# Packed attention with a feed-forward network: the first batch runs alone through all inner chunks

## The chip, the cores and the metric

The kernel runs on one core of a Trainium2 chip. The metric is the device time of one execution in microseconds (us), median of the runs. TensorE (PE) multiplies matrices into PSUM banks; VectorE (DVE), ScalarE (ACT) and GpSimd (POOL) work element by element; SyncE (SP) issues the transfers.

## The reference, cut to what matters

```python
def sm_attn(qq, kk, vv):                       # per batch and head
    s = scale * np.matmul(qq, kk.transpose(0, 1, 3, 2))
    s = s - np.max(s, axis=-1, keepdims=True)
    a = np.exp(s)
    a = a / (np.sum(a, axis=-1, keepdims=True) + 1e-09)
    return np.matmul(a, vv)
p_packed = sm_attn(p, k, v)                    # 32 packed rows per head
out = sm_attn(q, p_packed, p_packed)           # 576 tokens per head
...
h = x @ w_in                                   # x: 4608 x 512, w_in: 512 x 2048
g = h * (1.0 / (1.0 + np.exp(-1.702 * h)))
return (g @ w_out).astype(np.float32)          # w_out: 2048 x 512
```

There are 8 batches, 8 heads, 576 tokens a batch, heads of 64; the weights are float64 in memory.

## The kernel before, in words

All work is written out as one list of steps, `order` (from line 675), which is run from the top; it sets each engine's order. Engines meet only by semaphores. For a batch `b` the steps are:

- `load` brings k and the packed rows, q and v. Their tiles share two buffers, so q of a batch waits until k of it is used.
- `scores1`, the first softmax (`max1_first`, `bias1`, `exp1`, `sum1`), `turn1` (PE transposes the exps in 128-column pieces, plus the last 64) and `pack` (line 352) make the packed rows P; `pack_turn` transposes them to `PT`. Each exists for even and odd heads (`eo` 0 and 1).
- `scores2_mm`, `scores2_turn`, `max2`, `sub2`, `exp2`, `sum2`, `norm2`, `turn2` make the second softmax for one half of the tokens (288, `half` 0 and 1), both parities side by side in a tile of 576 columns.
- `m_chunk` (line 385) multiplies PT by one of four column chunks of w_in (512 columns), for even and odd heads in two banks. So the attention's product with w_in is never made in full: an `h_mm` step (line 539) multiplies the second softmax by that m.
- Every operand that is multiplied is split into an upper part that PE takes in its fast form and a lower part, the rest: `a_upper`/`a_lower`, `m_upper`/`m_lower`, `h_upper`/`h_lower` (tiles ghi, glo), `upper_w`/`lower_w`. One `h_mm` step is six matmuls of 288 columns for one 128-row slice `f` (16 of them) and one half of the tokens; one `out_mm` step is three matmuls of 512 columns for one `f` and one block of 128 tokens (four of them). In the head some lower parts are made by PE itself, with an identity and a negated identity, and copied (`a_lower_mm`, tile psal; `lower_w_mm`, tile pswl).
- `h_tanh` (ACT) and `h_gate` (DVE) make the gate. The last 64 tokens of each batch are kept aside (`h_over`) and multiplied for two batches at once (`over_mm`), then copied (`over_take`) and stored (`over_store`).

The weights come as 32 blocks of 128 rows in 64-bit form: 16 of w_in (four per chunk) and 16 of w_out (one per `f`), numbered as they are needed. `load_w` fetches a block, `begin_w` (ACT) and `join_w` (DVE) make 32-bit numbers of it; a block of w_out then needs `upper_w` and `lower_w`.

In the kernel before, the first two batches take turns. The table `spans` (line 663) lets batch 0 run chunk 0, batch 1 chunks 0 and 1, batch 0 chunks 1 to 3 and batch 1 chunks 2 and 3. The unfinished sums of a span are stored in device memory (`aside`) and fetched back (`back`) to be added at the end. So the attention of batch 1 stands in the head as well, between the first steps of batch 0. Where PE has nothing to do there, `warm` steps (line 121) multiply the identity by itself, with no use of the result. Every `warm` matmul shows as two instructions in the profile.

```python
spans = [(0, 0, 1), (1, 0, 2), (0, 1, 4), (1, 2, 4)]
```

Of the kernel before, what the change touches and what calls it, by code (L numbers as in the profile page):

```python
# [21 lines left out]
def kernel(  # L22
# [31 lines left out]

# [19 lines left out]
    DEC = 3  # L74
    SCALE = 1.0 / float(D) ** 0.5
# [6 lines left out]
    dram = ctx.enter_context(tc.tile_pool(name="dram", bufs=1, space=bass.MemoryType.DRAM))  # L82
# [90 lines left out]
    def load_w(n):  # L173
        w = queue[n]
        i = slot_of(w)
        if w[0] == "in":
            src, at = w_in_raw[w[2] * P : (w[2] + 1) * P, :], 4 * w[1] * FC
        else:
            src, at = w_out_raw[w[1] * P : (w[1] + 1) * P, :], 0
        raw[i] = wk.tile([P, DM, 2], U32, tag=f"wo{i}", name=f"raw{i}")  # L180
        halves = raw[i].rearrange("p n w -> p (n w)").bitcast(U16)
        nc.sync.dma_start(halves[:, : 4 * DM - 1], src[:, at + 1 : at + 4 * DM])
# [7 lines left out]
    tops = [cst.tile([P, DM], U32, name=f"top{i}") for i in range(DEC)]  # L190
# [5 lines left out]
    def begin_w(n):  # L196
        top[n] = tops.pop(0)
        nc.scalar.copy(
            top[n].bitcast(F16).rearrange("p (n h) -> p n h", h=2)[:, :, 1],
            raw[slot_of(queue[n])].bitcast(BF16).rearrange("p n (w h) -> p n w h", h=2)[:, :, 1, 0],  # L200
        )

    def join_w(n):
        w = queue[n]
        if w[0] == "in":
# [3 lines left out]
        nc.vector.scalar_tensor_tensor(  # L209
            dec[n].bitcast(U32), raw[slot_of(w)][:, :, 0], 13, top[n],  # L210
            op0=ALU.logical_shift_right, op1=ALU.bitwise_or,
        )
        tops.append(top[n])
# [138 lines left out]
    def pack(b):  # L352

        aT, vt = st["aT", b], kq["v", b]
        bank = bank_b(f"pspv_{b}")
        bv = bank[:, : 2 * D].rearrange("p (e d) -> p e d", d=D)
        for eo in range(2):
            for c in range(KC):
                kk = P if c < KC - 1 else KLAST
                for j in range(NP):  # L360
                    e0 = (2 * j + eo) * D
                    nc.tensor.matmul(  # L362
                        bv[32 * j : 32 * j + 32, eo, :],
                        aT[:kk, c, eo, 32 * j : 32 * j + 32],
# [20 lines left out]
    def m_chunk(b, fc, banks=(bank_b, bank_b)):  # L385

        PT = st["PT", b]
        banks = [bank(f"psm_{b}_{fc}_{eo}") for eo, bank in enumerate(banks)]
        for j in range(NP):
            for eo in range(2):  # L390
                nc.tensor.matmul(  # L391
                    banks[eo][32 * j : 32 * j + 32, :],
                    PT[rows(eo), j, :],
                    w_in_sb[fc][rows(eo), j, :],
                    start=True,
                    stop=True,
                )
        st["bank", "m", b, fc] = banks

    def m_upper(b, fc, eo, engine=nc.scalar):  # L400
        bank = st["bank", "m", b, fc][eo]
        hi = wk.tile([P, FC], F32R, tag=f"mhi{eo}", name=f"mhi_{b}_{fc}_{eo}", bufs=2)
        move(engine, hi, bank)
        st["m", b, fc, eo] = [hi, bank]

    def m_again(b, fc, banks):

        PT = st["PT", b]
        st["again", b, fc] = banks = [bank(f"psma_{b}_{fc}_{i}") for i, bank in enumerate(banks)]
        for j in range(NP):  # L410
            for eo in range(2):
                nc.tensor.matmul(
                    banks[eo][32 * j : 32 * j + 32, :],
                    PT[rows(eo), j, :],
                    w_in_sb[fc][rows(eo), j, :],
                    start=True,
                    stop=False,
                )
        for eo in range(2):
            hi = st["m", b, fc, eo][0]  # L420
            nc.tensor.matmul(banks[eo], minus, hi, start=False, stop=True)

    def m_again_copy(b, fc, eo, engine=nc.scalar):
        m = st["m", b, fc, eo]
        m[1] = wk.tile([P, FC], F32R, tag=f"mlo{eo}", name=f"mlo_{b}_{fc}_{eo}", bufs=2)
        move(engine, m[1], st["again", b, fc][eo])

    def m_lower(b, fc, eo):
        hi, bank = m = st["m", b, fc, eo]
        m[1] = wk.tile([P, FC], F32R, tag=f"mlo{eo}", name=f"mlo_{b}_{fc}_{eo}", bufs=2)  # L430
        nc.vector.tensor_tensor(m[1], bank, hi.bitcast(F32), op=ALU.subtract)  # L431
# [50 lines left out]
    def norm2(b, half):  # L482
        key = (2, b, half)
        x, rs = st["x", *key], st["rs", *key]
        nc.vector.tensor_tensor(groups(x), groups(x), over(rs), op=ALU.mult)

    def turn2(b, half):
        st["t", 2, b, half] = t = x_tile(f"xt_{b}_{half}")
        nc.vector.transpose(t, st["x", 2, b, half])

    def a_upper(b, half, engine=nc.scalar):
        t = st["t", 2, b, half]
        hi = wk.tile([P, S], F32R, tag="ahi", name=f"ahi_{b}_{half}", bufs=4)
        lo = wk.tile([P, S], F32R, tag="alo", name=f"alo_{b}_{half}", bufs=4)
        move(engine, hi, t)
        st["a", b, half] = (hi, lo)

    def a_lower_mm(b, half, banks):

        hi, lo = st["a", b, half]  # L500
        for eo in range(2):
            at = slice(eo * NH, (eo + 1) * NH)
            st["al", b, half, eo] = bank = banks[eo](f"psal_{b}_{half}_{eo}")
            t = st["t", 2, b, half][:, at]
            nc.tensor.matmul(bank[:, :NH], ident, t, start=True, stop=False)  # L505
            nc.tensor.matmul(bank[:, :NH], minus, hi[:, at], start=False, stop=True)

    def a_lower_copy(b, half, engine=nc.scalar):
        lo = st["a", b, half][1]
        for eo in range(2):  # L510
# [875 lines left out]
```

## Time and profile before

| what | value |
|---|---|
| median of 3 runs | 717.47 us (716.63 to 718.25) |
| the profiled execution, its own time | 716.67 us |
| span of the profiled execution | 714.9 us |
| PE busy | 706.4 us, 99% |
| DVE, ACT, POOL busy | 411.5, 271.9, 138.7 us |
| bytes moved by transfers | 60.06 MB |

The span runs from the first to the last instruction of the program; the own time holds what lies around it too. A row of instructions in time order gives its start, how long its group lasted, the engine, the source line, the operation, the tiles (out<-in), the shape and the count. A group by line or form gives the total busy time and the mean of one in ns, then the idle time before.

### The profile page before, as it was taken

How to read it: one execution, taken by the hardware profiler on the slowest of the kernel's cores; microseconds unless marked ns; L12 is line 12 of the kernel's file. 1: busy time of each engine (PE TensorE's matmuls, PEld its weight loads, DVE VectorE, ACT ScalarE, POOL GpSimd, SP SyncE). 2: the span in 40 equal slices, each digit the busy share in tenths (PEclk: the TensorE clock that was granted, in tenths of full speed). 3: DMA queues.
4: the chain of work that ended last, by engine and by line, in shares of the span. 5: the costliest groups of instructions: out<-in, count | busy, mean ns of one | idle time of the engine just before them, and what ended most of it. 6: DMA issues, size and time to landing. Idle time of an engine off the chain costs nothing.

```text
span 714.9 us, 13041 instructions
## 1 busy us (share of the span) xinstructions
PE 706.4 (99%) x5115; PEld 576.1 (81%) x5115; DVE 411.5 (58%) x1022; ACT 271.9 (38%) x653; POOL 138.7 (19%) x177
## 2 busy tenths in 40 slices
PE   8999999999999999999999999999999999999997
PEld 6678887887878878888887788888787887878885
DVE  4898766765834255335635467543673637855543
ACT  3666554533224344444223333442232333233330
POOL 1042222112232143322141112201241100000000
PEclk9999999999999999999999999999999999999999
DMA  8879063114122202121100400413013110010001
GB/s 315 323 280 349 34 244 119 33 47 147 51 83 71 70 2 107 53 67 71 67 16 1 123 26 1 143 35 119 1 23 110 37 54 1 1 60 0 1 11 63
DMA packets 18619, 60.06 MB, mean 84 GB/s; under 512 B 2176, under 2 KB 2176, under 8 KB 17536
## 3 DMA queue, kind: packets, MB, share of 16 engines
q1 hardware_dynamic: 18560, 59.25, 23.7%
q8 instruction: 40, 0.66, 0.4%
q14 instruction: 19, 0.16, 0.1%
HBM read 47.70 MB, written 11.53 MB: 83 GB/s over the span
## 4 chain that ended last, share of the span: by engine, by line
PE 96%; DVE 2%; DMA 1%; ACT 0%; POOL 0%; issue 0%; SPq 0%; DVEq 0%; ACTq 0%
PE acc L607 49%; PE h L547 29%; PE acc_over L607 6%; PE psm L391 4%; PE pspv L362 2%; PE ps L240 1%; PE ps L440 1%; PE pst L330 1%; PE warm L125 1%; DMA k<-pk 1%; PE psal L505 0%; POOL glo L534 0%; DVE wo L222 0%; DVE mx L287 0%; ACT x L117 0%; DVE aT L119 0%
## 5 line engine op out<-in xcount | busy, mean ns | idle before, releaser
L607 PE MATMUL acc<-wo,ghi 128*128 128x512 f32 x1024 | 323.7, 397 | 0.0
L607 PEld LDWEIGHTS acc<-wo,ghi 128*128 128x128 f32 x1024 | 179.8, 188 | 41.2 <-issue 14.9
L555 ACT ACTIVATE g<-h 128x288 f32<-128x288 f32 x256 | 103.8, 410 | 258.3 <-PE h L547 227.2
L607 PE MATMUL acc<-wo,glo 128*128 128x512 f32 x512 | 201.7, 394 | 0.1
L534 POOL TENSOR_TENSOR glo<-g,ghi 128x288 fp32r<-128x288 f32 (+1 forms) x153 | 115.5, 764 | 423.3 <-ACT ghi L117 221.4
L537 DVE SCALAR_TENSOR_TENSOR g<-g,h 128x288 f32<-128x288 f32 (+1 forms) x256 | 104.7, 415 | 129.0 <-ACT g L555 128.0
L547 PE MATMUL h<-ahi,mhi 128*128 128x288 f32 x512 | 145.8, 299 | 0.7 <-DVE g L537 0.4
L547 PE MATMUL h<-ahi,mlo 128*128 128x288 f32 x512 | 143.3, 295 | 0.0
L607 PEld LDWEIGHTS acc<-wo,glo 128*128 128x128 f32 x512 | 96.1, 188 | 23.4 <-POOL glo L534 1.1
L547 PE MATMUL h<-alo,mhi 128*128 128x288 f32 x512 | 110.3, 297 | 0.0
L547 PEld LDWEIGHTS h<-ahi,mhi 128*128 128x128 f32 x512 | 96.2, 188 | 17.1 <-DVE x L451 2.9
L547 PEld LDWEIGHTS h<-ahi,mlo 128*128 128x128 f32 x512 | 96.2, 188 | 7.0
L117 ACT CAST ghi<-g 128x288 fp32r<-128x288 f32 (+1 forms) x160 | 63.1, 406 | 61.0 <-DVE g L537 46.8
L547 PEld LDWEIGHTS h<-alo,mhi 128*128 128x128 f32 x512 | 82.1, 188 | 0.1
L537 DVE SCALAR_TENSOR_TENSOR over<-g,h 128x64 f32<-128x64 f32 x128 | 27.3, 214 | 65.7 <-ACT g L555 65.4
L534 DVE TENSOR_TENSOR glo<-g,ghi 128x224 fp32r<-128x224 f32 (+1 forms) x103 | 42.9, 425 | 12.1 <-ACT ghi L117 7.9
L431 DVE TENSOR_TENSOR mlo<-psm,mhi 128x512 fp32r<-128x512 f32 x64 | 43.1, 683 | 4.4 <-ACT mhi L117 4.0
L607 PE MATMUL acc_over<-wo,ghi_over 128*128 128x512 f32 x128 | 39.8, 392 | 0.0
L119 DVE CAST ghi<-g 128x224 fp32r<-128x224 f32 (+1 forms) x96 | 29.6, 314 | 13.4 <-PE acc_over L607 7.1
L391 PE MATMUL psm<-w_in,PT 64*32 64x512 f32 x512 | 35.5, 597 | 0.0
L117 ACT CAST mhi<-psm 128x512 fp32r<-128x512 f32 x44 | 25.3, 587 | 23.2 <-PE psm L391 23.1
L607 PEld LDWEIGHTS acc_over<-wo,ghi_over 128*128 128x128 f32 x128 | 23.6, 188 | 4.9 <-issue 0.2
(85 smaller groups left out, 494.1 us busy)
## 6 DMA issues: line engine op xcount, KB each, us to landing
q<-q SPq DMA_DIRECT2D x16, 576.0 KB, 5.4
v<-v SPq DMA_DIRECT2D x8, 1024.0 KB, 6.6
raw<-w_in SPq DMA_DIRECT2D x16, 511.8 KB, 10.4
raw<-w_out SPq DMA_DIRECT2D x16, 511.8 KB, 5.8
o<-o SPq DMA_DIRECT2D x24, 256.0 KB, 2.3
k<-pk SPq DMA_DIRECT2D x8, 640.0 KB, 4.4
k<-pk SPq DMA_DIRECT2D x8, 576.0 KB, 6.2
aside<-o SPq DMA_DIRECT2D x8, 256.0 KB, 4.5
```

Of the source, the lines that this page charges most:

```text
L117: nc.scalar.copy(dst, src)
L119: engine.tensor_copy(dst, src)
L125: nc.tensor.matmul(t[:, :P], ident, ident, start=True, stop=True)
L240: nc.tensor.matmul(bank[32 * j : 32 * j + 32, :NH], kq["p", b][rows(eo), j, :], kq["k", b][rows(eo), half, j, :], start=True, stop=True,)
L362: nc.tensor.matmul(bv[32 * j : 32 * j + 32, eo, :], aT[:kk, c, eo, 32 * j : 32 * j + 32], vt[:kk, c, e0 : e0 + D], start=(c == 0), stop=(c ...
L391: nc.tensor.matmul(banks[eo][32 * j : 32 * j + 32, :], PT[rows(eo), j, :], w_in_sb[fc][rows(eo), j, :], start=True, stop=True,)
L431: nc.vector.tensor_tensor(m[1], bank, hi.bitcast(F32), op=ALU.subtract)
L534: engine.tensor_tensor(lo, src, hi.bitcast(F32), op=ALU.subtract)
L537: nc.vector.scalar_tensor_tensor(dst, th, 1.0, h, op0=ALU.add, op1=ALU.mult)
L547: nc.tensor.matmul(h[:, :NH], m[eo][part][:, fo : fo + P], a[:, eo * NH : (eo + 1) * NH], start=(n == 0), stop=(n == len(terms) - 1),)
L555: nc.scalar.activation(g, st["h", b, f, half][:, :NH], AF.Tanh, scale=1.702)
L607: nc.tensor.matmul(acc, gp[:, at : at + P], wo[f][:, part, :], start=(start and i == 0), stop=(stop and i == 2),)
```

## The change

Batch 0 now runs through all four chunks before batch 1 begins them; `spans`, `aside` and `back` are gone, and each batch's sums stay in their four banks from `f` 0 to 15. Batch 1's first scores, turns, pack and second scores move behind output steps of batch 0. The four blocks of chunk 0 of w_in are loaded, decoded and multiplied in two column halves (`part` 0 and 1). The second softmax of batch 0's first 288 tokens runs for even and odd heads apart (`eo`), with its subtraction and its product (`norm2`) on POOL. `pack` of batch 0 writes its two parities into two banks. `lower_w` goes to POOL by default; no lower part of a weight and only two of the four lower parts of a (psal) are made on PE. Later batches have `sub2` and `norm2` on POOL in part, and all of their steps stand in a newly written order. There are 27 warm calls instead of 42. The last store is cut into column halves: DVE and ACT copy one each, SP stores one and ACT's own queue the other.

```diff
+    def columns(part):
+        return slice(0, FC) if part is None else slice(part * FC // 2, (part + 1) * FC // 2)
-    def load_w(n):
+    def load_w(n, part=None):
...
-        nc.sync.dma_start(halves[:, : 4 * DM - 1], src[:, at + 1 : at + 4 * DM])
+        at = columns(part)
+        a, e = 4 * at.start, 4 * at.stop - 1
+        nc.sync.dma_start(halves[:, a:e], src[:, a + 1 : e + 1])
...
-    tops = [cst.tile([P, DM], U32, name=f"top{i}") for i in range(DEC)]
+    tops = [cst.tile([P, DM], U32, name=f"top{i}") for i in range(4)]
...
-    def lower_w(n, engine=nc.vector):
+    def lower_w(n, engine=nc.gpsimd):
...
-    def pack(b):
+    def pack(b, eo=None, banks=(bank_b,)):
...
+    def m_mms(b, fc, banks, part, stop):
         PT = st["PT", b]
         for j in range(NP):
             for eo in range(2):
                 nc.tensor.matmul(
+                    banks[eo][32 * j : 32 * j + 32, columns(part)],
                     PT[rows(eo), j, :],
+                    w_in_sb[fc][rows(eo), j, columns(part)],
...
-    def sub2(b, half):
-        x, mx = st["x", 2, b, half], st["mx", 2, b, half]
-        nc.vector.tensor_tensor(groups(x), groups(x), over(mx), op=ALU.subtract)
+    def sub2(b, half, eo=None, engine=nc.vector):
+        x, mx = (even_odd(st[i, 2, b, half], eo) for i in ("x", "mx"))
+        engine.tensor_tensor(groups(x), groups(x), over(mx), op=ALU.subtract)
...
+    def norm2(b, half, eo=None, engine=nc.vector):
+        x, rs = (even_odd(st[i, 2, b, half], eo) for i in ("x", "rs"))
+        engine.tensor_tensor(groups(x), groups(x), over(rs), op=ALU.mult)
...
     def out_mm(b, f, i):
-        first, last = ends[b, f]
-        if first:
-            accs[i] = acc_bank(i, f"{b}_{f}")
-        product(accs[i], gs[b, f], f, i * P, first, last)
+        if f == 0:
+            accs[i] = acc_bank(i, f"{b}")
+        product(accs[i], gs[b, f], f, i * P, f == 0, f == NF - 1)
...
-    def over_take(pair, engine=nc.scalar):
-        taken["over"] = o_tile(f"o_over_{pair}")
-        move(engine, taken["over"], accs[0])
-
-    def over_store(pair, k):
-        at = (2 * pair + k + 1) * S - REST
-        nc.sync.dma_start(out[at : at + REST, :], taken["over"][k * REST : (k + 1) * REST, :])
+    def over_take(pair, k, engine=nc.scalar):
+        if k == 0:
+            taken["over"] = o_tile(f"o_over_{pair}")
+        move(engine, taken["over"][:, columns(k)], accs[0][:, columns(k)])
+
+    def over_store(pair, k, engine=nc.sync):
+        rows_ = out.rearrange("(b s) d -> b s d", s=S)[2 * pair : 2 * pair + 2, S - REST :, columns(k)]
+        engine.dma_start(rows_, taken["over"][:, columns(k)])
...
-        (warm, 9, 3), (warm, 10, 2), (warm, 19, 2), (load, "k", 0, 0), (scores1_first, 0, 0),
+        (load, "k", 0, 0), (load, "k", 0, 1), (warm, 9, 3), (warm, 4, 2), (scores1_first, 1, 0),
...
-        (over_store, 3, 1), (over_store, 3, 0),
+        (store, 7, 1), (over_take, 3, 0), (over_take, 3, 1, dve), (over_store, 3, 1, nc.scalar),
+        (over_store, 3, 0),
```

How the instructions stand on PE behind the first two h steps in the kernel before (pstl and pst are turns, pswl and psal lower parts made on PE, pspv the pack, pspt its turn, h the next h step):

```order
L341 MATMUL pstl_439<-ident,x_1_0_320 64x128
L341 MATMUL pstl_439<-ident,x_1_1_322 64x128
L227 MATMUL pswl_454<-dec,ident 128x512
L228 MATMUL pswl_454<-wo_434,minus 128x512
L330 MATMUL pst_1_458<-ident,x_1_1_322 128x128 x4
L362 MATMUL pspv_464<-v_397,aT_404 32x64 x40
L505 MATMUL psal_1_0_512<-xt_1_507,ident 128x288
L506 MATMUL psal_1_0_512<-ahi_1_509,minus 128x288
L505 MATMUL psal_1_1_515<-xt_1_507,ident 128x288
L506 MATMUL psal_1_1_515<-ahi_1_509,minus 128x288
L379 MATMUL pspt_536<-ident,pn_533 128x128
L547 MATMUL h_1_0_546<-ahi_1_509,mhi_0_0_291 128x288
```

On PE ahead of the first h step in the changed kernel (x, xt and a of batch 0's first tokens, even heads, then odd heads):

```order
L522 MATMUL psal_0_0_317<-xt_0_311,ident 128x288
L523 MATMUL psal_0_0_317<-ahi_0_314,minus 128x288
L124 MATMUL warm_320<-ident 128x128 x2
L124 MATMUL warm_335<-ident 128x128 x3
L124 MATMUL warm_345<-ident 128x128 x3
L522 MATMUL psal_0_1_354<-xt_0_311,ident 128x288
L523 MATMUL psal_0_1_354<-ahi_0_314,minus 128x288
L124 MATMUL warm_367<-ident 128x128 x3
L561 MATMUL h_0_1_373<-ahi_0_314,mhi_0_0_331 128x288
L561 MATMUL h_0_1_373<-ahi_0_314,mlo_0_0_332 128x288
```

The turns, the pack and its turn of batch 1 have left this place, the lower part of the weight and of batch 0's second tokens are no longer PE's, and warm calls stand between the even and the odd heads.

On POOL, the first instructions of the changed kernel that work on data (x of batch 0 with its maxima mx and reciprocal sums rs; wo a block of w_out, alo and glo lower parts); in the kernel before, POOL's first such instruction is a glo:

```order
L486 TENSOR_TENSOR x_0_0_241<-x_0_0_241,mx_0_0_259 128x288 x2
L501 TENSOR_TENSOR x_0_0_241<-x_0_0_241,rs_0_0_285 128x288
L486 TENSOR_TENSOR x_0_1_266<-x_0_1_266,mx_0_1_306 128x576
L501 TENSOR_TENSOR x_0_0_241<-x_0_0_241,rs_0_0_285 128x288
L229 TENSOR_TENSOR wo_360<-dec,wo_360 128x512
L530 TENSOR_TENSOR alo_1_400<-xt_1_388,ahi_1_399 128x576
L548 TENSOR_TENSOR glo_0_419<-g_0_0_415,ghi_0_418 128x288
L548 TENSOR_TENSOR glo_1_437<-g_0_1_395,ghi_1_436 128x288
```

Four softmax steps, a weight's lower part and a's lower part now stand ahead of that glo.

## Rows read from the trace of the kernel before

**Rows 1.** The page: busy time, share of the span and instructions of each engine.

```profile
PE 706.4 (99%) x5115; PEld 576.1 (81%) x5115; DVE 411.5 (58%) x1022; ACT 271.9 (38%) x653; POOL 138.7 (19%) x177
```

**Rows 2.** Stretches: length, busy by engine (count), PEclk, DMA share, GB/s.

```profile
0.00:29.13 29.13, 26.58 (x297) 18.66 (x298) 16.70 (x40) 12.58 (x30) 2.09 (x9) 1.00 0.85 304
...
29.13:114.00 84.87, 84.87 (x603) 69.26 (x601) 68.25 (x153) 51.60 (x114) 22.88 (x27) 1.00 0.66 244
...
250.00:700.00 450.00, 449.25 (x3167) 370.02 (x3166) 247.12 (x639) 156.12 (x384) 79.46 (x98) 1.00 0.14 45
```

**Rows 3.** PE's groups by line, warm calls: from 0 to 11, from 11 to 29.

```profile
L125 PE MATMUL warm<-ident 128*128 128x128 f32 x22 | 5.4, 435 | 1.4 <-POOL ident masks.py:199 1.4
...
L125 PE MATMUL warm<-ident 128*128 128x128 f32 x62 | 8.7, 283 | 0.0
```

**Rows 4.** PE in order of time, from 8 to 43 us.

```profile
8.45 2.07 PE L125 MATMUL warm<-ident 128*128 128x128 f32 x8
10.32 0.92 PE L330 MATMUL pst<-ident,x 128*128 128x128 f32 x4
...
16.42 0.71 PE L440 MATMUL ps<-q,PT 64*32 64x288 f32 x16
...
29.13 0.38 PE L547 MATMUL h<-ahi,mhi 128*128 128x288 f32 x1
...
30.01 0.29 PE L547 MATMUL h<-ahi,mhi 128*128 128x288 f32 x1
...
30.80 0.38 PE L341 MATMUL pstl<-ident,x 128*64 128x128 f32 x2
...
41.36 0.62 PE L607 MATMUL acc<-wo,ghi 128*128 128x512 f32 x2
...
42.05 0.62 PE L607 MATMUL acc<-wo,ghi 128*128 128x512 f32 x2
```

**Rows 5.** PE's groups by line, from 250 to 700 us (attention of four or five batches).

```profile
L440 PE MATMUL ps<-q,PT 64*32 64x288 f32 x160 | 7.0, 409 | 0.0
L362 PE MATMUL pspv<-v,aT 128*32 128x64 f32 (+1 forms) x320 | 7.0, 223 | 0.4 <-DVE aT L119 0.4
L240 PE MATMUL ps<-k 64*32 64x288 f32 x128 | 5.6, 405 | 0.0
L330 PE MATMUL pst<-ident,x 128*128 128x128 f32 x32 | 4.8, 272 | 0.0
```

**Rows 6.** Groups by form over the span, of ACT, DVE and POOL.

```profile
L198 ACT CAST top<-raw 128x512 f16<-128x512 bf16 x32 | 24.4, 781 | 4.0 <-DMA raw<-w_in 1.8 <-DVE w_in L209 1.4 <-DVE dec L209 0.8
L471 ACT ACTIVATE x<-x 128x576 f32<-128x576 f32 x16 | 10.9, 681 | 7.1 <-DVE x L467 7.0
...
L451 DVE STREAM_TRANSPOSE x<-ps 128x288 f32<-128x288 f32 x32 | 13.6, 460 | 15.3 <-PE ps L440 15.2
L467 DVE TENSOR_TENSOR x<-x,mx 128x576 f32<-128x576 f32 x16 | 12.9, 806 | 0.2
L209 DVE SCALAR_TENSOR_TENSOR dec<-raw,top 128x512 uint32<-128x512 uint32 x16 | 11.8, 740 | 0.2 <-ACT top L198 0.2
L516 DVE TENSOR_TENSOR alo<-xt,ahi 128x576 fp32r<-128x576 f32 x4 | 3.0, 756 | 0.1
...
L534 POOL TENSOR_TENSOR glo_over<-over,ghi_over 128x512 fp32r<-128x512 f32 x5 | 7.0, 1395 | 10.4 <-DVE ghi_over L119 8.1 <-ACT ghi_over L117 2.3
```

**Rows 7.** Transfers issued: KB each, median us to landing, first 16 us.

```profile
raw<-w_in SPq DMA_DIRECT2D x4, 511.8 KB, 9.3
```

**Rows 8.** The tile glo: shortest, median and longest ns by engine.

```profile
L534 POOL TENSOR_TENSOR glo<-g,ghi x153: 654/800/1277, 35.7 to 577.9; 128x288 fp32r<-128x288 f32 x79, 128x224 fp32r<-128x224 f32 x74
```

**Rows 9.** The end in order of time, of PE, DVE and SP.

```profile
709.77 0.40 PE L607 MATMUL acc_over<-wo,glo_over 128*128 128x512 f32 x1
...
710.26 0.69 DVE L119 COPY o_over<-acc_over 128x512 f32<-128x512 f32 x1 [6.53 <-PE acc_over L607]
...
710.98 1.11 SPq L659 DMA_DIRECT2D o<-o_over x2
```

More of the change, by code (lines that the diff above doesn't have):

```diff
@@ L74 @@
     DEC = 3
+    MB = 2
     SCALE = 1.0 / float(D) ** 0.5
@@ L423, in m_again_copy, with m_chunk @@
[L423 to L431, printed above, removed]
+    def m_chunk(b, fc, banks=(bank_b, bank_b), part=None):
+        banks = [bank(f"psm_{b}_{fc}_{eo}_{part}") for eo, bank in enumerate(banks)]
+        m_mms(b, fc, banks, part, True)
+        for eo in range(2):
+            st["bank", "m", b, fc, eo, part] = banks[eo]
@@ new lines, in m_upper, with m_lower @@
+    def m_upper(b, fc, eo, part=None, engine=nc.scalar):
+        if not part:
+            st["m", b, fc, eo] = [
+                wk.tile([P, FC], F32R, tag=f"{tag}{eo}", name=f"{tag}_{b}_{fc}_{eo}", bufs=MB)
+                for tag in ("mhi", "mlo")
+            ]
+        at = columns(part)
+        move(engine, st["m", b, fc, eo][0][:, at], st["bank", "m", b, fc, eo, part][:, at])
+    def m_lower(b, fc, eo, part=None):
+        at = columns(part)
+        hi, lo = (m[:, at] for m in st["m", b, fc, eo])
+        bank = st["bank", "m", b, fc, eo, part]
+        nc.vector.tensor_tensor(lo, bank[:, at], hi.bitcast(F32), op=ALU.subtract)
@@ new lines, in m_again, with m_again_copy @@
+    def m_again(b, fc, banks, part=None):
+        banks = [bank(f"psma_{b}_{fc}_{eo}_{part}") for eo, bank in enumerate(banks)]
+        m_mms(b, fc, banks, part, False)
+        at = columns(part)
+        for eo in range(2):
+            st["again", b, fc, eo, part] = banks[eo]
+            nc.tensor.matmul(
+                banks[eo][:, at], minus, st["m", b, fc, eo][0][:, at], start=False, stop=True
+            )
+    def m_again_copy(b, fc, eo, part=None, engine=nc.scalar):
+        at = columns(part)
+        move(engine, st["m", b, fc, eo][1][:, at], st["again", b, fc, eo, part][:, at])
@@ L498, in a_lower_mm @@
[L498 to L510, printed above, removed]
-            at = slice(eo * NH, (eo + 1) * NH)
-            move(engine, lo[:, at], st["al", b, half, eo][:, :NH])
+    def norm2(b, half, eo=None, engine=nc.vector):
+        x, rs = (even_odd(st[i, 2, b, half], eo) for i in ("x", "rs"))
+        engine.tensor_tensor(groups(x), groups(x), over(rs), op=ALU.mult)
@@ new lines, in turn2, with a_upper @@
+    def turn2(b, half, eo=None):
+        if not eo:
+            st["t", 2, b, half] = x_tile(f"xt_{b}_{half}")
+        t, x = (even_odd(st[i, 2, b, half], eo) for i in ("t", "x"))
+        nc.vector.transpose(t, x)
+    def a_upper(b, half, eo=None, engine=nc.scalar):
+        if not eo:
+            st["a", b, half] = [
+                wk.tile([P, S], F32R, tag=tag, name=f"{tag}_{b}_{half}", bufs=4)
+                for tag in ("ahi", "alo")
+            ]
+        t, hi = (even_odd(i, eo) for i in (st["t", 2, b, half], st["a", b, half][0]))
+        move(engine, hi, t)
@@ L514, in a_lower, with a_lower_mm, a_lower_copy @@
+    def a_lower_mm(b, half, eo, bank):
+        st["al", b, half, eo] = bank = bank(f"psal_{b}_{half}_{eo}")
+        t, hi = (even_odd(i, eo) for i in (st["t", 2, b, half], st["a", b, half][0]))
+        nc.tensor.matmul(bank[:, :NH], ident, t, start=True, stop=False)
+        nc.tensor.matmul(bank[:, :NH], minus, hi, start=False, stop=True)
+    def a_lower_copy(b, half, eo, engine=nc.scalar):
+        move(engine, even_odd(st["a", b, half][1], eo), st["al", b, half, eo][:, :NH])
     def a_lower(b, half, engine=nc.gpsimd):
```

1379 lines of the change are left out of this document (669 added, 710 removed).

## The prediction

> **What bounds the kernel now.** I read the engines' busy times first, then the stretches, then TensorE (PE) in order of time, then the prices of single operations, and the end last. PE is busy for 706.4 of 714.9 us [rows 1], and from 250 to 700 us for 449.25 of 450 [rows 2]. In between nothing can be gained unless PE's work shrinks, and it hardly does: the change keeps all 1,536 matmuls of the h steps, all 1,728 of the output and all of the attention, and only drops two residual pairs of 288 columns, one of 512, and 15 of 42 warm calls. So the change can act in three places: the head (0 to some 40 us), the new stretch in which the first batch runs alone, and the end.
>
> That PE is "busy" in the head misleads. A warm matmul computes nothing, and 84 of them stand there [rows 3]. The first h step begins at 29.13 [rows 4]. From there I price PE's two main steps by start to start: six matmuls of an h step take 0.79 (30.01 to 30.80), three of an output step 0.69 (41.36 to 42.05) [rows 4].
>
> **The head, measured at one milestone.** I take the moment at which six h steps are done. Before, that is 41.36 [rows 4], with one output step done and the whole attention of the second batch as well. That attention is the part that moves. Its groups cost per batch, from the steady stretch, 7.0/4 for pack, 5.6/4 for the first scores, 7.0/5 for the second and 4.8/4 for the turns [rows 5], 5.8 us of busy time. The small turns left out would add some 0.6, and the end of each group lies over the start of the next, some 0.1 at eight joints; I take 5.4, with 5.0 and 6.4 as bounds. The changed kernel has by my walk four output steps at its sixth h step. For that content the kernel before would have needed 41.36 - 5.4 + 3 x 0.69 = 38.0.
>
> Now the walk through the changed kernel, with prices of [rows 6] (half an operation is taken at 0.4 to 0.46, from the 288-element row):
>
> To the second scores. PE's eight warm rows from 8.45 to 10.32 that stand ahead of the first turns [rows 4] become six, placed ahead of the moment at which the exps are there: about 0.9 earlier. The pack is split by parity, into two banks, so its first half (0.87, half of 7.0/4) runs while the other parity's turns are copied: 0.9. The second scores move from 16.42 [rows 4] to 14.6. The transfers allow it: ahead of q stand three half blocks of w_in instead of three whole ones, 768 KB less by 511.8 KB a block [rows 7], and at the head's 304 GB/s [rows 2] that is 2.5 us.
>
> To the first h step. Before, this is 29.13 - 16.42 = 12.7 us, through whole-width softmax steps and four whole weight blocks. Now the even heads alone go scores 0.7, transpose 0.46, a weight join 0.4, max 0.4, subtraction on POOL 0.9, exp 0.4, sum and two small ones 0.8, product on POOL 0.9, and another transpose 0.45 behind the max of the other tokens: 20.5. The weights' first column halves are joined by about 19, and the half chunk ends near 19.6. From there ACT sets the pace, with eleven operations in its order: seven of 0.4 (three weight halves, the odd exp, the two upper parts of a, one lower part), two upper parts of m at 0.35, a whole weight at 0.78 and a whole exp at 0.68, 5.0 in all, of which 0.3 goes off for starts that overlap, to 24.3. Then the last residual pair on PE 0.5, its copy 0.4, and a rest of warm rows: the first h step starts at 25.4, 3.7 sooner.
>
> To the sixth h step. Work: 6 x 0.79, 4 x 0.69 and half an m chunk 0.5, 8.0 us. Waits that I find: 0.6 at the second half chunk (the third weight's right half is joined only at 27.6, behind the other tokens' softmax on VectorE), 0.3 at the third h step (its lower part of a comes from POOL), 0.3 at the first output step (glo from POOL). Sum 9.2, so 34.6. Against 38.0 that is **3.4 us gained**.
>
> POOL is the unknown in it. The trace has no subtraction with a broadcast operand on POOL. POOL's plain ones, of 288 and 224, have 0.80 as their median and 1.28 as their longest [rows 8], and on VectorE the broadcast form costs 806 against 756 for the plain one [rows 6], 7% more: 0.9, which I used. If all were like the longest, two such steps on the way to h and two behind it cost 0.9 more. The median speaks for many, the longest for one, so I take 0.3 off: **3.1**, with 2.2 and 4.2 as ends (the latter with the attention at 5.0 and ACT's order a little faster).
>
> **Work hidden beside PE.** The eight results set aside and fetched back, with their VectorE additions, go; they are beside PE, worth nothing. Ten lower parts of w_out and fourteen whole softmax steps' worth go from VectorE to POOL, and 28 glo pieces the other way; POOL is busy 19% of the span [rows 1], so nothing there either, unless a POOL result is late; then the next output step is late by 1 us at most. Parts of the weights in column halves add eight transfers, eight casts and eight joins, all in ACT's and VectorE's order above.
>
> **The end.** Before: the last matmul starts at 709.77, VectorE's copy of 512 takes 0.69 from 710.26, and SP issues two stores from 710.98 in 1.11 [rows 9]. Now each engine copies 256 columns (0.4), which saves 0.3, and each issues one store, which saves the second issue, 0.5. Against it stand packets of 1 KB instead of 2: nothing if only bytes count, 0.6 if a packet's time does not halve. The trace has no store from ACT's queue. So 0.8 at best and -0.1 at worst; I take **0.5**. The Trainium skill (DMA: Bandwidth & Descriptors, "Issuing engines are not separate DMA queues") says that transfers from several engines "will ultimately run on the same 16 DMA engines and interleave with each other", and that only the sequencer's time is saved. By that rule alone the end gains at most the 0.5 of issue and 0.3 of copy; no run so far shows a second queue.
>
> **Sum.** 3.1 + 0.5 = 3.6 us. The profiled execution took 716.67 (span 714.9), so 713.1 by it; the median of the runs shown, 717.47, lies 0.8 above, and gives **713.9 us**.
>
> **Rivals.**
> *The bill comes later.* Alone, the first batch needs all 32 weight blocks within one batch's 85 us of PE, where two batches shared them. VectorE was busy 68.25 of 84.87 us from 29.13 to 114 [rows 2], and by the two orders some six joins of 0.74 more fall into it now; a block that is late costs a join 0.74, an upper part of some 0.6 and a lower one of 1.4 on POOL [rows 6], 2.7 us, and one or two late ones eat the gain: 716.6 to 719.3. For it: VectorE and ACT work in a fixed order, so one late block holds what is queued behind it. Against: 73 us in 85 still fit, and the walk shows every block of the second chunk landed 3 us or more before it is cast. Chance 0.22; half of it ends under 716.0, as a loss of 1 to 2 us only.
>
> *The clock.* This is the case on the slower side. Warm matmuls took 435 ns on the mean in the first 11 us and 283 after [rows 3], the same form, so PE ran at its lower level first and rose around 11 us, after scores, warm calls and turns with hardly a gap. The column of the granted clock reads 1.00 for all of the head [rows 2], so only the rows tell. The changed kernel has 15 warm calls fewer, and in my walk PE idles for 1 us at a time between 17.6 and 24. If the clock rises only with the h steps, the 5 us of PE work on the way double in part (+2.5), and the first 6 us of h and output steps run at half pace (+3): 713.9 + 5.5 = 719.4. It decides if the rise is later than about 25 us. The Trainium skill (TensorE: Matmul & The Clock Gate, "The HAM clock gate") states that "the default state is throttled, and activity releases the throttle", which speaks against thinner warm work. Against it: from the first scores to the pack PE is as gapless as before, so a rise near 11 us is likelier, and no idle stretch in the walk is over 1.5 us. Chance 0.10, of which 0.06 ends over 718.9.
>
> *Nothing comes of it.* The early h steps only wait longer at the first output steps, since wo's lower part and glo both come from POOL and stand behind a's; PE reaches its stream no sooner, and 716.5 to 717.5 is left after the end's 0.5. For it: POOL has eight operations in a row there. Against: their sum is 9 us from 17 to 31. Chance 0.08.
>
> **Chances and range.** Forecast 0.60, the bill 0.22, the clock 0.10, nothing 0.08. A measurement tells 0.2% (1.4 us) from no change. Faster by more: 0.60 + 0.07 + 0.03 = 0.70; same: 0.10 + 0.03 + 0.06 = 0.19; slower: 0.05 + 0.06 = 0.11 (the bill splits 0.07, 0.10, 0.05, the clock 0.03, 0.03, 0.04, and 0.02 of nothing goes slower). The forecast's own range is 712.4 to 715.5, from the ends of the two terms and 0.5 for steady work reordered; out to the bill's usual price it is 711.9 to 717.3.
>
> **What would show it.** Right: first h step near 25.4, sixth done near 34.6, PE without gaps from there to the end, last matmul about 3 us sooner, 4.2 instead of 4.7 us behind it. Wrong: warm rows over 300 ns after 15 us (clock); PE waiting for wo or w_in between 35 and 115 (the bill); POOL's subtractions over 1.3 us; gaps in the stream of later batches, whose order is also new.

## The result, and the profile after

The changed kernel takes 720.85 us (median of 20 runs, 718.14 to 723.35), the kernel before 717.18 in the same comparison: a ratio of 1.0052, 95% interval 1.0039 to 1.0065. It is 3.7 us slower; 713.9 was forecast, with a range up to 717.3. The profiled execution took 720.04 us, with a span of 718.3.

PE does less work in a longer span (against [rows 1]; the page's line of busy times):

```profile
PE 698.7 (97%) x5092; PEld 567.6 (79%) x5092; DVE 410.1 (57%) x1030; ACT 275.7 (38%) x666; POOL 147.4 (21%) x173
```

The stretches, in the columns of [rows 2], now parted at the new first h step. The head is 2.7 us shorter, POOL works 6.43 us in it, and the transfers are busy for 0.95 of it. The steady stretch is as full as before.

```profile
0.00:26.43 26.43, 19.11 (x231) 12.48 (x232) 14.09 (x42) 12.33 (x34) 6.43 (x15) 1.00 0.95 351
26.43:114.00 87.57, 84.91 (x643) 68.29 (x641) 77.16 (x161) 54.35 (x119) 42.26 (x39) 1.00 0.49 179
250.00:700.00 450.00, 449.59 (x3155) 369.27 (x3142) 249.67 (x647) 160.74 (x393) 65.68 (x80) 1.00 0.14 46
```

PE in order of time, changed kernel, against [rows 4]: second scores of the first and of the other tokens, first h step, the two parts of the second half chunk, the third h step, the first output step, the sixth h step and the output step behind it.

```profile
14.90 0.72 PE L451 MATMUL ps<-q,PT 64*32 64x288 f32 x16 [0.66 <-DMA q<-q]
18.13 0.72 PE L451 MATMUL ps<-q,PT 64*32 64x288 f32 x16 [1.65 <-DMA q<-q]
...
26.43 0.38 PE L561 MATMUL h<-ahi,mhi 128*128 128x288 f32 x1
...
28.21 0.64 PE L399 MATMUL psm<-w_in,PT 64*32 64x256 f32 x8
30.62 0.64 PE L399 MATMUL psm<-w_in,PT 64*32 64x256 f32 x8 [1.77 <-DVE w_in L217]
31.18 0.40 PE L561 MATMUL h<-ahi,mhi 128*128 128x288 f32 x1
...
32.09 0.62 PE L621 MATMUL acc<-wo,ghi 128*128 128x512 f32 x2
...
36.27 0.30 PE L561 MATMUL h<-ahi,mhi 128*128 128x288 f32 x1
...
37.07 0.62 PE L621 MATMUL acc<-wo,ghi 128*128 128x512 f32 x2
```

So six h steps are done at 37.07, not at 34.6. And the end in order of time, against [rows 9]: the last matmul starts 1.1 us earlier than before (708.68 against 709.77), and all is lost behind it. From its end to the span's end it is 718.3 - 709.07 = 9.2 us, where it was 714.9 - 710.17 = 4.7.

```profile
708.68 0.39 PE L621 MATMUL acc_over<-wo,glo_over 128*128 128x512 f32 x1
709.15 0.37 ACT L116 COPY o_over<-acc_over 128x256 f32<-128x256 f32 x1 [14.69 <-PE acc_over L621]
709.55 0.53 SPq L659 DMA_DIRECT2D o<-o_over  x1
709.56 0.42 DVE L118 COPY o_over<-acc_over 128x256 f32<-128x256 f32 x1 [6.94 <-ACT o_over L116]
710.02 1.14 ACTq L659 DMA_DIRECT2D o<-o_over  x1
```

The view of transfers shows why. First the kernel before, from 710 to 715 us: GB/s in 40 slices, packets, and the queue that carried them.

```profile
GB/s 0 0 0 0 0 0 0 0 0 0 0 0 0 0 0 0 66 197 213 246 213 115 246 213 246 164 148 33 0 0 0 0 0 0 0 0 0 0 0 0
DMA packets 160, 0.26 MB, mean 52 GB/s; under 512 B 32, under 2 KB 32, under 8 KB 160
...
q1 hardware_dynamic: 160, 0.26, 23.7%
```

Then the changed kernel from 709 to 718.3 us, with the share of 16 engines that were busy (in tenths) as the first line:

```profile
DMA  0000000011111110111111111111111110000000
GB/s 0 0 0 0 0 0 0 26 18 35 44 18 44 40 22 31 48 48 44 53 44 48 48 48 48 48 48 48 48 48 48 48 48 31 0 0 0 0 0 0
DMA packets 260, 0.26 MB, mean 28 GB/s; under 512 B 4, under 2 KB 260, under 8 KB 260
...
q1 hardware_dynamic: 130, 0.13, 4.9%
q10 hardware_dynamic: 130, 0.13, 4.0%
```

The same 0.26 MB go at 48 GB/s instead of 213 to 246, with a tenth of the engines busy. Before, there were 128 packets of data and 32 under 512 B, 16 for each of two stores. Now 256 packets of data come with 4 small ones, two for each store. If each engine that takes part sends one small packet, two engines do each store. The share of busy engines fits this: from 711 to 717 us it is 0.12 to 0.14, and two of 16 are 0.125. The new store's address pattern is batches (2) by rows (64) by columns (256), so its outermost size is 2; that of the old one was 64 rows. Nor do the two stores run side by side, though ACT issued its own at 710.02: from 709 to 714 us only SP's queue moves packets (first line), from 714.3 to the end only ACT's (second line).

```profile
q1 hardware_dynamic: 123, 0.13, 8.7%
q10 hardware_dynamic: 121, 0.12, 8.6%
```

### The profile page after: what moved, and what is told of

Read it like the earlier page. It is cut to its first block, busy times and chain, and to the rows that moved or that the text cites. A ratio compares the mean times of both kernels' runs of the same rounds, so it can differ in the third digit from the quotient of the medians.

```text
span 718.3 us, 12990 instructions
## 1 busy us (share of the span) xinstructions
PE 698.7 (97%) x5092; PEld 567.6 (79%) x5092; DVE 410.1 (57%) x1030; ACT 275.7 (38%) x666; POOL 147.4 (21%) x173
## 4 chain that ended last, share of the span: by engine, by line
PE 93%; DMA 2%; DVE 2%; issue 1%; POOL 1%; ACT 1%; SPq 0%; POOLq 0%; ACTq 0%; DVEq 0%
PE acc L621 50%; PE h L561 28%; PE acc_over L621 6%; PE psm_None L399 4%; PE pspv L370 1%; PE ps L247 1%; DMA q<-q 1%; PE ps L451 1%; PE pst L337 1%; DMA k<-pk 1%; DVE w_in L217 0%; POOL glo L548 0%; DVE mx L294 0%; PE pstl L348 0%; ACT x L116 0%
## 5 line engine op out<-in xcount | busy, mean ns | idle before, releaser
L548 POOL TENSOR_TENSOR glo<-g,ghi 128x288 fp32r<-128x288 f32 (+1 forms) x125 | 96.6, 783 | 303.0 <-ACT ghi L116 190.0
L621 PEld LDWEIGHTS acc<-wo,glo 128*128 128x128 f32 x512 | 96.1, 188 | 25.4 <-POOL glo L548 1.9
L116 ACT CAST ghi<-g 128x288 fp32r<-128x288 f32 (+1 forms) x155 | 60.9, 406 | 61.5 <-DVE g L551 39.0
L548 DVE TENSOR_TENSOR glo<-g,ghi 128x224 fp32r<-128x224 f32 (+1 forms) x131 | 56.6, 443 | 17.5 <-ACT ghi L116 14.8
L427 DVE TENSOR_TENSOR mlo<-psm_None,mhi 128x512 fp32r<-128x512 f32 x62 | 42.1, 684 | 5.0 <-ACT mhi L116 4.6
L116 ACT CAST mhi<-psm_None 128x512 fp32r<-128x512 f32 x44 | 25.7, 587 | 31.5 <-PE psm_None L399 31.5
L118 DVE CAST ghi<-g 128x224 fp32r<-128x224 f32 (+1 forms) x101 | 33.2, 336 | 5.9 <-PE acc L621 2.4
L399 PE MATMUL psm_None<-w_in,PT 64*32 64x512 f32 x496 | 34.0, 596 | 0.0
```

What stands on the lines that cost most here:

```text
L116: nc.scalar.copy(dst, src)
L118: engine.tensor_copy(dst, src)
L399: nc.tensor.matmul(banks[eo][32 * j : 32 * j + 32, columns(part)], PT[rows(eo), j, :], w_in_sb[fc][rows(eo), j, columns(part)], start=True ...
L427: nc.vector.tensor_tensor(lo, bank[:, at], hi.bitcast(F32), op=ALU.subtract)
L548: engine.tensor_tensor(lo, src, hi.bitcast(F32), op=ALU.subtract)
L621: nc.tensor.matmul(acc, gp[:, at : at + P], wo[f][:, part, :], start=(start and i == 0), stop=(stop and i == 2),)
```

## The experiments

All "ratios" are to the kernel before, from runs on the same chip. "Behind the last matmul" is counted from its end, 0.39 us after its start.

**The end: form, packets or queue.** Four kernels; the theory is the form of the store, the rivals are packets of 1 KB, ACT's queue, and the stream.

```diff
 # e1
-(over_take, 3, 0), (over_take, 3, 1, dve), (over_store, 3, 1, nc.scalar), (over_store, 3, 0),
+(over_take_whole, 3, dve), (over_store_rows, 3, 1), (over_store_rows, 3, 0),
```

The two steps of e1 are the last copy and store of the kernel before.

> The changed kernel with the last copy and store of the kernel before (one copy of 512 columns on VectorE, two stores of 64 whole rows from SP). If the loss lies in the new store alone, 4.7 us follow the last matmul's end instead of 9.2, the span is 718.3 - 4.5 = 713.8, and the kernel is faster than before by the head's gain of about 1.1 us, ratio 0.998 to 0.999. If the time were lost in the stream of the batches, the ratio would stay at 1.004 or more.

Measured: 715.8 us, ratio 0.9984 (0.9969 to 0.9999); span 713.5, 4.9 us behind the last matmul. With the old end the kernel is no longer slower than before: the loss lies in the end alone.

```profile
708.24 0.39 PE L621 MATMUL acc_over<-wo,glo_over 128*128 128x512 f32 x1
```

```diff
 # e2
+    def over_store_cols(pair, k, engine=nc.sync):
+        for i in range(2):
+            at = (2 * pair + i + 1) * S - REST
+            engine.dma_start(out[at : at + REST, columns(k)], taken["over"][i * REST : (i + 1) * REST, columns(k)])
...
-(over_store, 3, 1, nc.scalar), (over_store, 3, 0),
+(over_store_cols, 3, 1, nc.scalar), (over_store_cols, 3, 0),
```

> The changed kernel, its column halves kept, but each half stored as two transfers of 64 rows x 256 columns (packets of 1 KB as in the change), two from SP and two from ACT. If the store is slow because its outermost size is 2 (one entry for each batch, so that two transfer engines do all of it), the packets now spread over all engines and 4.5 to 5.5 us follow the last matmul. If packets of 1 KB are slow as such, 8 us or more stay. If ACT's queue is the slow part, SP's two land early and ACT's last, 7 us in all.

Measured: 714.95 us, ratio 0.9978 (0.9967 to 0.9989); span 713.1, 4.5 us behind the last matmul. The transfers of e2 from 708 to 714 us:

```profile
GB/s 0 0 0 0 0 0 0 0 0 0 0 0 0 0 41 191 171 34 150 184 273 205 130 232 123 14 0 0 0 0 0 0 0 0 0 0 0 0 0 0
DMA packets 320, 0.26 MB, mean 44 GB/s; under 512 B 64, under 2 KB 320, under 8 KB 320
...
o<-o_over SPq DMA_DIRECT2D x2, 64.0 KB, 2.2
o<-o_over ACTq DMA_DIRECT2D x2, 64.0 KB, 2.1
```

The same 256 packets of 1 KB, the same two queues, but four stores with 16 small packets each, and up to 273 GB/s. So packets of 1 KB are not slow as such, and ACT's queue is not either (2.1 us to landing against SP's 2.2).

```diff
 # e3
-(over_store, 3, 1, nc.scalar),
+(over_store, 3, 1),
```

> The changed kernel with both column halves stored from SP's queue, in the change's form. If the form is the cause, nothing is mended: each store still takes 2.7 to 3.5 us, one behind the other, and 8.7 to 9.7 us follow the last matmul. If the second queue is the cause (ACT's start, or two queues in turn), 5 to 6 us follow.

Measured: 721.72 us, ratio 1.0062 (1.0045 to 1.008); span 718.8, 9.7 us behind the last matmul. One queue instead of two changes nothing that counts: the form decides.

```profile
708.76 0.39 PE L621 MATMUL acc_over<-wo,glo_over 128*128 128x512 f32 x1
```

```diff
 # e4, in the kernel before
-(over_take, 3, dve), (over_store, 3, 1), (over_store, 3, 0),
+(over_take_cols, 3, 0), (over_take_cols, 3, 1, dve), (over_store_cols, 3, 1, nc.scalar), (over_store_cols, 3, 0),
```

> The kernel before with the change's last copy and store alone. If the end costs by itself, whatever runs ahead of it, 9.2 us follow the last matmul instead of 4.7 and the span is 714.9 + 4.5 = 719.4, ratio 1.006. If the loss needs the changed stream ahead of it, the ratio stays within 1.002.

Here `over_take_cols` and `over_store_cols` are the changed kernel's own `over_take` and `over_store`, not the store of e2.

Measured: 722.08 us, ratio 1.0075 (1.0062 to 1.0089); span 720.2, 9.1 us behind the last matmul. The end costs 4.4 us by itself. The last matmul starts 0.9 us later than before, too, but that stands already at the sixth h step (done at 42.30 against 41.36), so it is not the end's.

```profile
710.68 0.40 PE L607 MATMUL acc_over<-wo,glo_over 128*128 128x512 f32 x1
```

**The head: why 1.1 us instead of 3.1.** VectorE and POOL of the changed kernel, in order of time:

```profile
26.26 0.36 DVE L217 SCALAR_TENSOR_TENSOR w_in<-raw,top 128x256 uint32<-128x256 uint32 x1
...
28.91 1.66 DVE L217 SCALAR_TENSOR_TENSOR w_in<-raw,top 128x256 uint32<-128x256 uint32 x1
```

```profile
27.05 1.39 POOL L229 TENSOR_TENSOR wo<-dec,wo 128x512 fp32r<-128x512 f32 x1 [2.96 <-ACT wo L116]
28.88 1.41 POOL L530 TENSOR_TENSOR alo<-xt,ahi 128x576 fp32r<-128x576 f32 x1 [0.44 <-ACT ahi L116]
```

The same join of 256 columns takes 0.36 alone and 1.66 where it begins just behind POOL's alo; it ends 0.28 after alo does, as if it had stood still until then. This join is what PE waits 1.77 us for at 30.62. Two kernels test it, both on top of e2:

```diff
 # h1
-(a_lower, 0, 1),
+(a_lower, 0, 1, dve),
```

> The changed kernel with the stores of the run e2, and one more word: the lower part of a for the first batch's other tokens goes from POOL to VectorE, right ahead of the weight join that took 1.66 us. If that join was long because POOL worked at the time (POOL's alo stood from 28.88 to 30.29, the join from 28.91 to 30.57), it falls to 0.4 us, the second part of m's half chunk starts 0.4 to 0.5 earlier than 30.62, and the third h step likewise (31.18 to some 30.7). If the join is long by itself (its data, its place), it stays at 1.3 us or more, and that half chunk starts at about 31.4, 0.75 later, by the added step on VectorE.

Measured: 714.37 us, ratio 0.9968 (0.9951 to 0.9985). The join, now behind VectorE's own alo, with POOL idle:

```profile
28.43 0.75 DVE L530 TENSOR_TENSOR alo<-xt,ahi 128x576 fp32r<-128x576 f32 x1
29.10 0.41 DVE L217 SCALAR_TENSOR_TENSOR w_in<-raw,top 128x256 uint32<-128x256 uint32 x1
```

```diff
 # h2
-(join_w, 1, 1), (lower_w, 4),
+(join_w, 1, 1), (join_w, 2, 1), (lower_w, 4),
...
-(join_w, 2, 1), (m_chunk, 0, 0, (bank_b, bank_b), 1),
+(m_chunk, 0, 0, (bank_b, bank_b), 1),
```

> The changed kernel with the stores of the run e2, and the same weight join (third block, right half) placed ahead of the other tokens' product and transpose on VectorE, where POOL does nothing. By the theory that POOL's work stretches it, it takes 0.4 us there, PE no longer waits 1.77 us at the half chunk, and the third h step is held by POOL's alo alone: about 30.7 instead of 31.18. By the theory that it is long by itself, it takes 1.3 us or more, the transposed other tokens are later by that, and the third h step starts at 31.5 or later.

Measured: 714.35 us, ratio 0.9957 (0.9941 to 0.9973). Two joins in 0.69 on VectorE, and on PE the half chunk in one piece:

```profile
25.08 0.69 DVE L217 SCALAR_TENSOR_TENSOR w_in<-raw,top 128x256 uint32<-128x256 uint32 x2
```

```profile
27.00 0.66 PE L399 MATMUL psm<-w_in,PT 64*32 64x256 f32 x16
28.65 0.37 PE L561 MATMUL h<-ahi,mhi 128*128 128x288 f32 x1 [0.99 <-DVE g L551]
```

The start of the head differs by up to 2 us between profiles. In seven of these eleven the first h step stands 8.3 to 8.5 us behind the other tokens' scores, so it follows the landing of q's second half, which differs (below). The places are therefore compared from the first h step on: to the start of the third, to the end of the sixth and to the start of the last matmul.

| run | other tokens' scores | first h step | to the third | to the sixth's end | to the last matmul | lower clock, between | span |
|---|---|---|---|---|---|---|---|
| changed kernel | 18.13 | 26.43 | 4.75 | 10.64 | 682.25 | | 718.3 |
| e1 | 16.63 | 24.93 | 5.07 | 11.66 | 683.31 | 29 and 33 | 713.5 |
| e2 | 16.19 | 24.70 | 4.74 | 11.79 | 683.48 | 30 and 34 | 713.1 |
| e3 | 17.00 | 25.30 | 4.75 | 10.62 | 683.46 | | 718.8 |
| h1 | 16.30 | 26.06 | 4.07 | 9.96 | 681.55 | 21 and 25 | 712.6 |
| h2 | 16.95 | 25.25 | 3.40 | 9.81 | 681.46 | | 711.7 |
| h3 | 17.54 | 26.05 | 4.76 | 11.80 | 683.55 | 31 and 36 | 714.6 |
| h4 | 18.59 | 26.41 | 4.06 | 10.06 | 681.72 | | 713.1 |
| b1 | 17.30 | 25.81 | 3.39 | 9.80 | 681.54 | | 712.3 |
| b2 | 16.19 | 26.51 | 3.39 | 9.80 | 681.62 | | 713.1 |
| b4 | 16.72 | 25.58 | 3.40 | 9.80 | 681.41 | | 711.9 |

Two things set these times apart. One is the join: moved, with alo left on POOL (h2, b1, b2, b4), the sixth is done after 9.80, where the changed kernel and e3 need 10.6. That is 0.8 us, and between the changed kernel and h2 it is still there at the last matmul.

The other is PE's clock. In e1, e2, h1 and h3 the granted clock fell to the lower of its two levels (1.2 and 2.4 GHz) inside the head and rose again; the column says between which times. The same columns as in [rows 2], for the changed kernel, e1, e2, h1 and h3:

```profile
29.00:33.00 4.00, 2.14 (x17) 1.30 (x17) 3.88 (x8) 2.71 (x7) 2.57 (x3) 1.00 1.02 409
29.00:33.00 4.00, 3.89 (x19) 2.92 (x20) 2.81 (x9) 2.38 (x6) 2.79 (x3) 0.57 1.02 408
30.00:34.00 4.00, 4.00 (x17) 3.30 (x16) 3.61 (x8) 2.33 (x7) 4.00 (x4) 0.57 0.87 349
21.00:25.00 4.00, 4.00 (x20) 3.80 (x20) 3.63 (x11) 3.04 (x8) 1.13 (x2) 0.57 1.03 411
31.00:36.00 5.00, 5.00 (x23) 4.25 (x23) 4.48 (x10) 3.33 (x9) 4.27 (x4) 0.66 0.58 231
```

The third h step of e1 lasts 1.61 us up to the output step behind it, that of the changed kernel 0.91. So 1.1 to 1.3 us of the time to the last matmul in e1, e2 and h3 go with the clock and not with their edits. (e3 has no fall, but one wait of 0.97 for a gate at 68.52.) Before the fall PE had waited 1.8 us for the join in e1, e2 and h3, and 1.0 for a transpose in h1; but the changed kernel and e3 wait just as long without a fall, so what sets it off is open.

Runs whose trace was not kept show it in their mean granted clock. Behind the last matmul PE is idle and the clock falls too, but this end, 9.2 of 718.3 us, can bring the mean no lower than 0.994 by itself. Eight of the changed kernel's 20 runs lie below that, at 0.988 to 0.992, with a median of 722.7 us; the other twelve have 719.7. In e1, where the shorter end brings it no lower than 0.997, four of eleven runs lie at 0.994 to 0.995, with a median of 717.8; the other seven have 714.8. The kernel before, in its 20 runs beside e1, lies at 0.997 to 1.000. Where the clock fell in those runs is not known.

Other edits of the head:

```diff
 # h3: VectorE's transpose that waits for q's second half
-(scores2_mm, 0, 1, late), (scores2_turn, 0, 1, 1),
+(scores2_mm, 0, 1, late),
...
-(join_w, 2, 0), (m_chunk, 0, 0, early, 0), (scores2_turn, 0, 1, 0),
+(join_w, 2, 0), (scores2_turn, 0, 1, 1), (m_chunk, 0, 0, early, 0), (scores2_turn, 0, 1, 0),
```

> The changed kernel with the stores of the run e2, and on VectorE the transpose of the other tokens' scores, which waits for q's second half, stands behind the even heads' sum and the third weight's join instead of ahead of them. If q's second half, landed at 18.1 us, holds the head through VectorE's order, POOL's first product starts at 19.1 to 19.4 instead of 20.38 and the first h step at 25.9 to 26.1 instead of 26.43. If ACT's order sets the pace, the first product moves but the first h step stays within 0.15 of 26.43.

Measured: 716.04 us, ratio 0.9983 (0.9974 to 0.9992). POOL's first product came at 19.68, the first h step at 26.05, with the scores themselves at 17.54. The h step lies where the expectation had it, but only because q came 0.6 us earlier than in the changed kernel; from the scores on it took 8.5 us instead of 8.3: nothing gained, no faster than e2.

> All three edits of the head together, and the last two copies into tiles of their own, so that VectorE need not wait for ACT's. If the causes add up, the third h step starts at 29.6 to 30.1 instead of 31.18, and the last copy ends 0.4 earlier: in all 1.0 to 1.5 us under the run e2, ratio to the kernel before 0.996. If the head is held by the transfers as a whole (the engines of the transfers are busy without a gap from 5 to 32 us), the third h step starts earlier, but the next ones wait for weights, and less than 0.5 us is left at the end.

The edits of h1, h2 and h3, and `over_take` into two tiles. Measured: 715.8 us, ratio 0.9981 (0.9966 to 0.9995): they don't add. With alo on VectorE and the join ahead of it, PE waits 1.64 us ahead of the third h step, now for a gate on VectorE. Four of the twelve runs have a mean clock of 0.992 to 0.994 and take 716.9 to 718.5; the other eight have a median of 714.7, near h2's 714.35. The profile of h4 had the latest q of all (18.59). In it VectorE's last copy still began only when ACT's was over, so a tile of its own is not what it lacks:

```profile
708.61 0.37 ACT L116 COPY o_over<-acc_over 128x256 f32<-128x256 f32 x1 [14.71 <-PE acc_over L621]
709.01 0.42 DVE L118 COPY o_over<-acc_over 128x256 f32<-128x256 f32 x1 [6.99 <-ACT o_over L116]
```

Three more on top of h2:

```diff
 # b1
-(begin_w, 26), (join_w, 26), (h_lower, 0, 9, 1, dve),
+(begin_w, 26), (h_lower, 0, 9, 1, dve), (join_w, 26),
 # b2
-(load, "q", 0, 0), (load_w, 1, 0), (join_w, 0, 1), (load, "q", 0, 1),
+(load, "q", 0, 0), (load, "q", 0, 1), (load_w, 1, 0), (join_w, 0, 1),
...
-(join_w, 1, 0), (max2, 0, 0, 0),
+(max2, 0, 0, 0),
...
-(max2, 0, 0, 1),
+(max2, 0, 0, 1), (join_w, 1, 0),
 # b4: b1 and b2
```

> The run h2 with two steps exchanged on VectorE near 74 us: the lower part glo that PE waits for there (a wait of 0.7 us in the changed kernel at 77.3 us) ahead of a weight join instead of behind it. If VectorE was only late because POOL's work beside it stretched a cast (1.18 us instead of 0.28) and the two joins (1.90 us for both), the glo comes 0.6 to 0.9 earlier and the wait of 0.7 goes: 0.5 to 0.7 us under h2 in PE's stream. If PE would be held by the next thing anyway (the join that is now later feeds the last column chunk), the wait turns up at that chunk and nothing is gained.

Measured: 714.01 us, ratio 0.996 (0.9946 to 0.9975). The wait is gone, and yet the time is that of h2: from the first h step to the last matmul 681.54 us against 681.46. That nothing is gained was expected in the second half of the text above; a wait at the next chunk, which it names as the reason, doesn't show. In the changed kernel the place looks as follows, VectorE first: a cast of 288 columns in 1.18 us while POOL makes a weight's lower part.

```profile
74.89 1.18 DVE L118 CAST ghi<-g 128x288 fp32r<-128x288 f32 x1
75.99 1.90 DVE L217 SCALAR_TENSOR_TENSOR w_in<-raw,top 128x512 uint32<-128x512 uint32 x2
77.81 0.38 DVE L548 TENSOR_TENSOR glo<-g,ghi 128x224 fp32r<-128x224 f32 x1
```

```profile
74.62 1.28 POOL L229 TENSOR_TENSOR wo<-dec,wo 128x512 fp32r<-128x512 f32 x1
```

> The run h2 with both halves of q issued ahead of the second weight block's left half (256 KB that no longer stand ahead of q's second half), whose join moves behind the even heads' maxima. If PE's wait for q's second half (0.5 to 2.1 us in the profiles so far) comes from the bytes ahead of it, at the 365 GB/s of this stretch 256 KB are 0.7 us: the wait falls to 0.2 or less and the first h step to about 24.7 (h2: 25.25). If the delay comes from elsewhere (engines of the transfers that lag at random), it stays between 0.5 and 2.

Measured: 715.12 us, ratio 0.997 (0.9958 to 0.9981). PE no longer waits for q's second half, but 0.85 us twice for the weights that q passed; the first h step comes at 26.51:

```profile
19.18 0.62 PE L399 MATMUL psm<-w_in,PT 64*32 64x256 f32 x4 [0.86 <-DVE w_in L217]
20.65 0.64 PE L399 MATMUL psm<-w_in,PT 64*32 64x256 f32 x8 [0.85 <-DVE w_in L217]
```

> Both of these edits. If they add, 1.0 to 1.3 us under h2: ratio to the kernel before 0.994 to 0.995. If the q edit does nothing, as b1.

Measured: 714.65 us, ratio 0.996 (0.9948 to 0.9972): as h2. By these profiles the head needs q and four half blocks at the same time through transfers that are busy for 0.95 of it, and their order only changes which of them is late; a kernel with fewer bytes there was not run.

## Why the prediction was wrong

**The end: 0.5 us gained was forecast, 4.5 lost.** The step that failed is the bound: "0.8 at best and -0.1 at worst", with packets of 1 KB as the only cost. It priced the size of a packet (at 0.6, for which no row is shown) and not how many engines send them. The diff's address pattern, outermost size 2, was there to see. The Trainium skill (DMA: Bandwidth & Descriptors, "Why a DMA increments its semaphore by 16 and not by 1") states that a transfer uses the largest number of engines up to 16 that divides the sizes of both sides' slowest dimension larger than one, here 2; the trace agrees, with 4 small packets for two stores where e2's four stores have 64, and 48 against up to 273 GB/s. The page that the prediction quoted held that rule too; the section on issuing engines was the wrong one to weigh. What was forecast of queues and copies mattered little: e2's end, with the good form, needs 4.5 us instead of 4.7. The halved copies save nothing: they run one after the other, 0.37 and 0.42, where the whole took 0.69.

**The head: 3.1 forecast, 1.1 measured** (e1, 0.1 to 2.2 by its interval; 2.3 by the median of its seven runs with the higher clock). The sum went wrong behind the first h step. Up to there the walk held: second scores at 14.90 (14.6 forecast), the first h step at 24.70 to 26.51 in eleven profiles (25.4; late where q landed late, as in the changed kernel and h4, or weights did, as in b2, or the clock fell, as in h1). From the first to the third h step the walk had some 3 us; with the join in its place the profiles have 4.74 to 4.76, and 5.07 in e1, where the clock fell. There "0.6 at the second half chunk" was 1.77, since the join took 1.66 and not 0.4. POOL "is the unknown in it", said the prediction, but it looked for the danger in POOL's own times, which were better than feared (0.67 instead of 0.9 for a subtraction). What it missed is that POOL's work holds up VectorE's. h2, which only moves this join to where POOL is idle, gives the size of the term: 0.8 us from the first h step on. (Its ratio of 0.9957, 3.1 us, is no measure of it: 0.2 of that is e2's end, and it comes from four runs.) The fall of the clock is the other part: between the two groups of e1's runs lie 3.0 us, and it lowers the gain by their median from 2.3 to 1.1. Also, three output steps stand ahead of the sixth h step, not four, so the milestone was 0.7 too good to begin with.

**The rivals.** The clock, as the prediction had it, did not come: a rise behind 25 us. Warm rows of the changed kernel took 281 ns from 15 to 27 us, and from 33.29 to 34.09 an h step takes 0.80 as before. But the clock fell again in four of eleven profiles and, by their mean, in eight of the changed kernel's 20 runs. The prediction leaned on "no idle stretch in the walk is over 1.5 us"; the wait for the join was 1.77. This did not decide the sign: the twelve other runs still have 719.7, above the range, and e4 loses 4.4 us at its end with the granted clock at 1.00 up to 709 us. (The prediction's chance for the clock to end over 718.9 is 0.06 in the rival and 0.04 in its split.) The bill came as one wait of 0.55 us at 78.2 us, which b1 removed without gain; it doesn't explain 3.7 us. (What held the gate in e3 was not followed up.) The rival on the slower side was looked for in the head, where the change is large; the loss sat in its smallest part.

**Sum.** 713.9 forecast and 720.85 measured are 7.0 apart: 5.0 at the end (4.5 lost for 0.5 gained) and 2.0 in the head. Of these 2.0 some 0.8 are the join's and some 1.1 the clock's, an estimate from h2 and from e1's two groups of runs.

**Open.** Why q's second half lands at 16 to 18.6 us is not settled; b2, with q first, spread over 0.8 us in five runs, where the changed kernel's runs spread over 5.2 and those of before over 2.2. Part of this spread goes with the clock, but what makes the clock fall in some runs and not in others is not settled either. Nor is it settled what makes VectorE's last copy wait for ACT's.

## What to carry to other kernels

Look at the outermost size of a transfer's address pattern before counting its bytes: four stores over 64 rows were 4.7 us faster at the end than two whose outermost size was 2. Before a step goes to POOL because POOL is idle, look at what VectorE does beside it, and place VectorE's two-operand steps where POOL is not at work. Price the last transfer of a kernel as carefully as its head, since nothing hides it. And read the granted clock of each profile and each run before a difference of 1 us is put down to an edit.

## What the runs showed of the hardware

- A store whose outermost size is 2 went at 48 GB/s and with two small packets, stores whose outermost size is 64 at up to 273 and with 16, for the same packets of 1 KB. Two such slow stores ran one behind the other, from one queue (9.7 us behind the last matmul) as from two (9.2).
- The granted clock can fall back after it has risen: to the lower level within 21 to 36 us in four of eleven profiles, at a cost of 1.1 to 1.3 us in three of them (e1, e2, h3).
- POOL's elementwise work stops some of VectorE's: a join of two operands took 0.36 us alone and 1.66 beginning just behind a POOL step of 1.41, a cast 1.18 beginning behind one of 1.28. The Trainium skill (SBUF — State Buffer, "SBUF: two separate sides") describes a port pair that VectorE and GpSimd hold in turn for a whole instruction; the traces agree, and h1 and h2 show that the join is short again once POOL is idle. The kernel before very likely had it as well: two joins from 35.49 us on took 1.90 together, with POOL's glo from 35.66 to 36.85 beside them, and the longest of its 16 joins of this form took 1302 ns (shortest, median, longest ns):

```profile
L209 DVE SCALAR_TENSOR_TENSOR dec<-raw,top x16: 677/686/1302, 29.5 to 148.6; 128x512 uint32<-128x512 uint32 x16
```
